# Reordering the beginning of a retention-plus-MLP kernel: table load, PSUM banks, early state terms, transfer order and half-width first columns

## The chip, the cores and the metric

One core of a Trainium2 chip runs the whole program. The metric is device microseconds for one execution. Engine names are those of the profile: PE (TensorE matmul), PEld (TensorE weight load), DVE (VectorE), ACT (ScalarE), POOL (GpSimd), SP (the engine that only issues transfers here).

## The reference

Inputs: q, k and v of 8 batches x 8 heads x 576 positions x 64, and two matrices, w_in (512 x 2048) and w_out (2048 x 512), all float32.

```python
scores = scale * np.matmul(q, k.transpose(0, 1, 3, 2))
gamma = 1.0 - 2.0 ** (-5.0 - np.arange(H))
Dmat = np.where(rel >= 0, gamma[:, None, None] ** rel[None, :, :], 0.0)   # rel = i - j
attn_out = np.matmul(scores * Dmat[None], v)                              # [8, 8, 576, 64]
x = attn_out.transpose(0, 2, 1, 3).reshape(B * S, H * D)                  # [4608, 512]
h = x @ w_in
out = (h * np.cos(h)) @ w_out                                             # [4608, 512]
```

The decay is a product of a factor of the query's position and one of the key's position, so the first part can be run as linear attention in chunks: within a chunk of 128 positions by masked scores, across chunks by a running 64 x 64 state for each head.

## The kernel before, in words

The program is written out by hand, instruction by instruction; there is no scheduler that moves anything. Each engine runs its own instructions in the order in which `emit` records them. The class `Sched` puts a wait in front of an instruction when a buffer (`Buf`) that it reads or writes was last touched by another engine. So the order of calls in `emit` is the order on every engine, and an instruction that waits holds up all that stands behind it on its engine.

**The long part.** The 4608 tokens are handled in 9 blocks of 512. For each block, `mlp1` makes 16 row tiles of h: four matmuls of 512 columns into one PSUM bank, then a cosine on ACT (a Sin with a bias of pi/2), then a product on DVE into `GT`. `mlp2` multiplies by w_out. The attention work of the next batches is put between these matmuls. There are eight PSUM banks: `mm0` to `mm3`, `sc0`, `sc1`, `po`, `st`.

**The beginning** is batch 0, and the change is only there (about 22 µs). It runs as follows.

- `load0` issues four pieces of k and four of q on SP (one for each pair of heads c), then `load` four chunks of v.
- `consts_a`, `consts_b`, `consts_n` make the masks and decay factors. `consts_b` runs four exponentials on ACT (the `up` factors, one for each c), and one buffer object, `bUP`, stands for all four. Behind them ACT loads a second function table for Sin (a one-element activation at line 694).
- `cast0` on POOL casts each piece to bf16 as it lands (k0, q0, k1, q1, ...). `vmul` on POOL multiplies each v chunk by its factors. Between these, `w_in_load` and `w_out_load` issue the matrices' transfers on POOL's queue, which also cast them to bf16. `WI` says how w_in's 16 column tiles are split over them: before, pieces of 2, 2, 4, 4 and 4 tiles.
- On PE, for each c: `turn0("k", c)` transposes k by 18 small matmuls, `back0(c - 1)` turns the result back into rows for the state, `turn0("q", c)` transposes q, `scores0(c - 1)` makes the masked scores of a pair of heads (eight matmuls, then two products on DVE at line 472). k's copies out of PSUM are on ACT (line 434, and 449 for `back0`), q's products with `up` on DVE (line 430). `spin(n, bank)` is n matmuls of the identity with itself, whose result nobody reads.
- `state(0, r)` adds chunk r to the running state in bank `st` and copies it out by two ACT instructions (line 585, buffer `SB[r]`). `sums(0, r)` makes chunk r's output: four matmuls of q with the state up to chunk r - 1, then eight of the masked scores with v; then one copy into `XT` (line 566), on ACT for even r and DVE for odd r.
- The fifth chunk of v and batch 1's k and v are loaded on SP behind the landing of w_in's last piece (`after=[w]`).
- Then come the 16 `mlp1` of block 0 and its `mlp2`.

Banks before: k's turns and `back0` go alternately to `mm0` and `mm1`, all q turns to `mm2`, the spins mostly to `st`.

Of the kernel before, what the change touches and what calls it, by code (L numbers as in the profile page):

```python
# [15 lines left out]
CH = 128  # L16
# [6 lines left out]
SP1 = 3 * 64 + CH  # L23
TQ = NP * S_
TP = 2 * TQ
WI = (0, 2, 4, 8, 12, 16)
NWO = 4


def ck_of(r):  # L30
    return min(CH, S_ - CH * r)
# [93 lines left out]
class _Kernel:  # L125
    def __init__(self, nc, es, q, k, v, w_in, w_out, out):
# [7 lines left out]
        def sb(name, shape, dt):  # L134
# [49 lines left out]
        self.MK = sb("mk", [128, CH], BF16)  # L184
        self.ID = sb("ident", [128, 128], BF16)
        self.LNG = sb("lng", [128, NP], F32)
        self.JUNK = sb("junk", [128, 1], F32)
        self.C_LN8 = sb("c_ln8", [128, 1], F32)
        self.C_PIH = sb("c_pih", [128, 1], F32)
        self.bIG, self.bIP, self.bUP, self.bWV, self.bMK, self.bC, self.bID, self.bUPN, self.bLW = (  # L190
            Buf() for _ in range(9))

        def ps(name):
            return nc.alloc_psum_tensor(name, [128, 512], F32)
# [31 lines left out]
    def consts_a(self):  # L226

        s = self.s
        s.op("pool", lambda e: e.iota(self.IP.ap(), [[CH, NCH]], base=0, channel_multiplier=1,
                                      allow_small_or_imprecise_dtypes=True), writes=[self.bIP])  # L230
        for t, b, fill, first, cmp in ((self.ID, self.bID, 1.0, 0.0, ALU.not_equal),
                                       (self.MK, self.bMK, 0.0, 1.0, ALU.is_ge)):
            s.op("dve", lambda e: e.memset(t.ap(), first), writes=[b])
            s.op("pool", lambda e: e.affine_select(t.ap(), t.ap(), pattern=[[1, CH]],
                                                   compare_op=cmp, fill=fill, base=0,
                                                   channel_multiplier=-1), reads=[b], writes=[b])
        for h in range(H_):
# [22 lines left out]
    def consts_b(self, c):  # L260

        s = self.s
        if c == 0:
            s.op("pool", lambda e: e.iota(self.IG.ap(), [[1, S_]], base=0, channel_multiplier=0,  # L264
                                          allow_small_or_imprecise_dtypes=True), writes=[self.bIG])
        s.op("act", lambda e: e.activation(  # L266
            bass.AP(self.UP, c * S_, [[NP * S_, 128], [1, S_]]), self.IG.ap(), AF.Exp,
            bias=self.C_LN8.ap(), scale=bass.AP(self.LNG, c, [[NP, 128], [1, 1]])),
            reads=[self.bIG, self.bC], writes=[Buf()])
        self.bUP.w = [Tok("act", "act", s.count["act"], {})]  # L270

# [138 lines left out]
    def turn_q(self, b, c, bank):  # L410
        s, i, n = self.s, b % 2, 9 * D_
        m, bm = bank
        f = self.turn9(m, lambda hp, t: bass.AP(
            self.QX[i], 64 * hp * NP * n + c * n + t * D_, [[NP * n, 64], [1, D_]]),
            [self.bQX[i]], bm)
        o = bass.AP(self.KQT[i], TQ + c * S_, [[TP, 128], [9, 64], [1, 9]])
        done = s.op("dve", lambda e: e.tensor_tensor(o, f, self.up9(c), ALU.mult),
                    reads=[bm, self.bUP], writes=[Buf()])
        for bq in self.bQT[i]:
            bq.w.append(done)  # L420

# [2 lines left out]
    def turn0(self, x, c, bank, eng):  # L424
        s, (m, bm) = self.s, bank
        f = self.turn9(m, lambda hp, t: self.rows0(x, c, 64, [t * D_, [1, D_]], hp),
                       [self.bX0[x][c]], bm)
        o = bass.AP(self.KQT[0], TQ * (x == "q") + c * S_, [[TP, 128], [9, 64], [1, 9]])
        if x == "q":
            fn = lambda e: e.tensor_tensor(o, f, self.up9(c), ALU.mult)  # L430
        elif eng == "dve":
            fn = lambda e: e.tensor_copy(o, f)
        else:
            fn = lambda e: e.activation(o, f, AF.Copy)  # L434
        done = s.op(eng, fn, reads=[bm] + [self.bUP] * (x == "q"), writes=[self.bT0[x][c]])
        for b in (self.bQT if x == "q" else self.bKT)[0]:
            b.w.append(done)

# [90 lines left out]
    def rest(self, b, r, po=None, eng="dve"):  # L529

        done = self.sums(b, r, po, eng)
        if r < NCH - 1:
            self.state(b, r)
        done()

    def sums(self, b, r, po=None, eng="dve"):

        s, ck, i, q0 = self.s, ck_of(r), b % 2, CH * r
        po, bpo = po or (self.PO, self.bPO)
        mms = []  # L540
        if r:
            sb = self.SB[(r - 1) % 3]
            mms += [(bass.AP(po, c * CH, [[512, 128], [1, ck]]),
                     bass.AP(sb, c * 128, [[512, 128], [1, 128]]),
                     bass.AP(self.KQT[i], TQ + c * S_ + q0, [[TP, 128], [1, ck]]),
                     dict(start=c == 0, stop=False, skip_group_check=True)) for c in range(NP)]
        for c in range(NP):
            for hp in range(2):
                h = 2 * c + hp
# [7 lines left out]
            reads += [x for bs in self.bR0 for x in bs]  # L557
        else:
            reads += self.bRT[self.rt[b, r]]
        if r:  # L560
            reads += [self.bSB[(r - 1) % 3], self.bQT[i][r]]
# [7 lines left out]
    def state(self, b, r):  # L569

        s, ck, i = self.s, ck_of(r), b % 2
        mms = []
        for c in range(NP):
            for hp in range(2):
                h = 2 * c + hp
                mms.append((
                    bass.AP(self.ST, 64 * hp * 512 + c * D_, [[512, 64], [1, D_]]),
                    bass.AP(self.KQB[i], 2 * DM * r + h * D_, [[NCH * 2 * DM, ck], [1, D_]]),
                    bass.AP(self.VB[i][r], h * D_, [[DM, ck], [1, D_]]),
                    dict(start=r == 0 and c == 0, stop=r == NCH - 2 and c == NP - 1,  # L580
                         skip_group_check=True)))
        self.group(mms, [self.bKB[i][r], self.bVB[i][r]], [self.bST])
        for hp in range(2):

            s.op("act", lambda e: e.activation(  # L585
                bass.AP(self.SB[r % 3], 64 * hp * 512 + 64 * hp, [[512, 64], [128, NP], [1, D_]]),
                bass.AP(self.ST, 64 * hp * 512, [[512, 64], [D_, NP], [1, D_]]), AF.Copy),
                reads=[self.bST], writes=[self.bSB[r % 3]] if hp else [Buf()])

    def stage(self, b, r):  # L590
        self.rest(b, r)
# [90 lines left out]
    def emit(self):  # L682
# [8 lines left out]
            self.consts_b(c)  # L691
        self.consts_n()

        s.op("act", lambda e: e.activation(self.JUNK.ap(), self.C_PIH.ap(), AF.Sin), reads=[self.bC])  # L694
        for c in range(NP):
            for x in "kq":
                self.cast0(x, c)
        self.vmul("pool", 0, 0)
        self.w_in_load(0)
        self.vmul("pool", 0, 1)  # L700
        self.vmul("pool", 0, 2)
        self.w_in_load(1)
        self.vmul("pool", 0, 3)
        for i in range(2, len(WI) - 1):
            w = self.w_in_load(i)
        for i in range(NWO):
            self.w_out_load(i)
            if i == 1:
# [2 lines left out]
        po, st = (self.PO, self.bPO), (self.ST, self.bST)  # L711
        mm, sc = list(zip(self.MM, self.bMM)), list(zip(self.SC, self.bSC))
        sc = [sc, [po, mm[3]]]
        self.spin(30, st)
        for c in range(NP):
            self.turn0("k", c, mm[c % 2], "act" if c else "dve")
            if c:
                self.back0(c - 1, mm[(c - 1) % 2])
            else:
                self.spin(4, st)  # L720
            self.turn0("q", c, mm[2], "dve")
            self.spin(4, st)
            if c:
                self.scores0(c - 1, sc[(c - 1) % 2])
        self.back0(3, mm[1])
        self.spin(8, mm[0])
        self.state(0, 0)
        self.scores0(3, sc[1])
        self.spin(4, mm[0])
        self.state(0, 1)  # L730
        self.spin(14, mm[2])
        self.state(0, 2)
        self.spin(14, mm[2])
        for r, bank in enumerate((mm[0], mm[1], mm[2], sc[0][0])):
            self.sums(0, r, bank, ("act", "dve")[r % 2])()
        self.state(0, 3)
        self.spin(6, po)
        self.n_mm = 3
        self.load("v", 0, NCH - 1, after=[w])
        self.vmul("pool", 0, NCH - 1)  # L740
# [3 lines left out]
        for r in range(NCH):  # L744
            self.casts(1, r)

        for dt in range(16):
            self.mlp1(0, dt)

        self.fetch(2)  # L750
# [96 lines left out]
```

## Time and profile before

| what | value |
|---|---|
| median of 3 runs (lowest to highest) | 314.74 µs (314.06 to 317.02) |
| the profiled execution's own time | 314.3 µs |
| its span, first to last instruction | 312.6 µs, so 1.7 µs lie around it |
| granted TensorE clock, mean | 1.00 |
| PE / PEld / DVE / ACT / POOL busy | 96% / 52% / 57% / 51% / 34% of the span |
| first `mlp1` weight load of block 0 | 22.09 µs from the span's start |
| PE busy before 22.09 µs | 17.58 of 22.09 µs |
| PE busy from 22.09 µs to the end | 283.92 of 290.51 µs |

Times inside the profile are microseconds from the span's start. A row of the timeline gives start, duration, engine, line, operation, output and inputs, and in brackets how long the engine was idle before and what released it. A row of the chain of waits gives start, duration and the work that the end of the program hung on at that moment; "issue" is time in which an engine waited for nothing that the profile shows. A row of a group gives the busy sum, the mean duration in ns, then the idle time before.

### The profile page before, as it was taken

Reading aid. Unit: us, or ns where it says so; the run is one execution under the profiler, and the core shown is the slowest. Engines: PE = TensorE matmul, PEld = TensorE weight load, DVE = VectorE, ACT = ScalarE, POOL = GpSimd, SP = SyncE. Lnnn points to the kernel's source line nnn. Section 1 sums busy time; section 2 is a strip of 40 time slices with the busy share of each in tenths; the row PEclk is TensorE's granted clock in tenths of the full one; section 3 lists DMA queues with packets and bytes.
Section 4 is the critical chain, followed back from the end, with each engine's and each line's share of the span. In section 5 each row is a group of like instructions: output and inputs, shape, how many; then the busy total and the mean of one; then the engine's idle time right before and its main releaser. Section 6 shows DMA issues by size and latency. Waiting matters only on the chain.

```text
span 312.6 us, 6548 instructions
## 1 busy us (share of the span) xinstructions
PE 301.5 (96%) x2578; PEld 162.2 (52%) x2614; DVE 176.8 (57%) x311; ACT 160.3 (51%) x283; POOL 107.8 (34%) x131
## 2 busy tenths in 40 slices
PE   7799999999999999999999999999999999999996
PEld 6564455666554555445544554455445554444444
DVE  4737644786547852685458554764487438405700
ACT  6657505775447533762367235723573247416711
POOL 5890017654657455645454654510000000000000
DMA  7999999999999999999999999940001100020012
GB/s 249 224 133 197 194 204 227 272 191 190 244 236 193 223 233 228 230 192 241 198 239 202 237 235 221 184 118 36 34 2 60 43 34 2 34 101 3 1 73 95
DMA packets 138846, 48.85 MB, mean 156 GB/s; under 512 B 127936, under 2 KB 133312, under 8 KB 138816
## 3 DMA queue, kind: packets, MB, share of 16 engines
q1 hardware_dynamic: 128352, 34.35, 58.3%
q0 software_dynamic: 5280, 4.78, 9.8%
q10 hardware_dynamic: 5184, 9.31, 8.2%
q8 instruction: 20, 0.33, 0.5%
q14 instruction: 10, 0.08, 0.1%
HBM read 36.70 MB, written 9.44 MB: 148 GB/s over the span
## 4 chain that ended last, share of the span: by engine, by line
PE 94%; ACT 3%; issue 2%; POOL 0%; DVE 0%; ACTq 0%
PE mm L491 63%; PE mm L493 21%; PE po L491 6%; PE sc L491 3%; PE st L491 2%; ACT up L266 1%; ACT L694 0%; ACT L266 0%; ACT kqb L449 0%; ACT sb L585 0%; DVE xt L566 0%; POOL ig L264 0%; ACT kqt L434 0%; PE st L493 0%; ACT osb L668 0%
## 5 line engine op out<-in xcount | busy, mean ns | idle before, releaser
L615 DVE TENSOR_TENSOR gt<-mm,cb 128x512 bf16<-128x512 f32 (+2 forms) x160 | 101.1, 637 | 62.4 <-ACT cb L612 61.1
L612 ACT ACTIVATE cb<-mm,c_pih 128x512 bf16<-128x512 f32 (+2 forms) x160 | 102.0, 644 | 30.3 <-PE mm L493 30.1
L491 PE MATMUL mm<-xt,win 128*128 128x512 bf16 (+2 forms) x470 | 116.6, 358 | 0.6 <-DVE xt L566 0.5
L491 PE MATMUL mm<-wout,gt 128*128 128x512 bf16 (+1 forms) x424 | 111.6, 372 | 3.0 <-issue 2.7
L491 PEld LDWEIGHTS mm<-xt,win 128*128 128x128 bf16 x480 | 45.5, 98 | 49.0 <-DVE gt L615 0.6
L491 PEld LDWEIGHTS mm<-wout,gt 128*128 128x128 bf16 x450 | 40.9, 98 | 42.0 <-DVE gt L615 0.2
L493 PE MATMUL mm<-xt,win 128*128 128x512 bf16 (+2 forms) x160 | 57.2, 358 | 0.4
L493 PE MATMUL mm<-wout,gt 128*128 128x512 bf16 (+1 forms) x142 | 53.6, 377 | 0.3
L649 ACT ACTIVATE osb<-mm 128x512 f32<-128x512 f32 x35 | 20.9, 597 | 62.8 <-PE mm L493 62.8
L339 POOL TENSOR_TENSOR vb<-vn,wv 128x512 bf16<-128x512 f32 (+1 forms) x40 | 41.6, 1041 | 30.0 <-DMA vn<-in_v_dram 28.2
L566 DVE CAST xt<-po 128x512 bf16<-128x512 f32 (+1 forms) x36 | 22.7, 630 | 41.8 <-PE po L493 41.8
L585 ACT ACTIVATE sb<-st 64x256 bf16<-64x256 f32 x64 | 24.1, 376 | 35.7 <-PE st L493 34.4
L339 POOL TENSOR_TENSOR kqb<-qn,upn 128x512 bf16<-128x512 f32 (+1 forms) x30 | 31.2, 1041 | 17.7 <-DMA qn<-in_q_dram 17.5
L350 POOL CAST kqb<-kn 128x512 bf16<-128x512 f32 (+1 forms) x35 | 21.3, 608 | 45.7 <-DMA kn<-in_k_dram 42.4
L518 DVE TENSOR_TENSOR rt<-sc,mk 128x512 bf16<-128x512 f32 (+1 forms) x52 | 29.2, 596 | 4.7 <-PE sc L493 4.7
L493 PEld LDWEIGHTS mm<-xt,win 128*128 128x128 bf16 x160 | 15.7, 98 | 15.7
L493 PEld LDWEIGHTS mm<-wout,gt 128*128 128x128 bf16 x142 | 13.9, 98 | 16.6
L491 PE MATMUL po<-rt,vb 128*64 128x128 bf16 (+1 forms) x252 | 14.0, 220 | 0.0
L518 DVE TENSOR_TENSOR rt<-mm,mk 128x512 bf16<-128x512 f32 x20 | 12.8, 678 | 0.0
L491 PEld LDWEIGHTS po<-kqt,sb 128*128 128x128 bf16 x116 | 8.3, 98 | 6.8 <-DVE rt L518 0.4
L491 PEld LDWEIGHTS po<-rt,vb 128*64 128x64 bf16 (+1 forms) x252 | 8.6, 108 | 5.6 <-DVE rt L518 2.1
L491 PE MATMUL po<-kqt,sb 128*128 128x128 bf16 (+1 forms) x116 | 10.4, 212 | 0.0
(115 smaller groups left out, 167.4 us busy)
## 6 DMA issues: line engine op xcount, KB each, us to landing
out_dram<-osb ACTq DMA_DIRECT2D x35, 256.0 KB, 3.4
vn<-in_v_dram SPq DMA_DIRECT2D x32, 256.0 KB, 5.4
kn<-in_k_dram SPq DMA_DIRECT2D x28, 256.0 KB, 4.5
qn<-in_q_dram SPq DMA_DIRECT2D x24, 256.0 KB, 4.8
wout<-in_moe_w_out_dram POOLq DMA_DIRECT2D x4, 512.0 KB, 18.4
win<-in_moe_w_in_dram POOLq DMA_DIRECT2D x3, 512.0 KB, 9.1
kn<-in_k_dram SPq DMA_DIRECT2D x4, 288.0 KB, 4.5
qn<-in_q_dram SPq DMA_DIRECT2D x4, 288.0 KB, 4.8
```

The costliest lines, as they stand in the source:

```text
L266: s.op("act", lambda e: e.activation(bass.AP(self.UP, c * S_, [[NP * S_, 128], [1, S_]]), self.IG.ap(), AF.Exp, bias=self.C_LN8.ap(), scal ...
L339: self.s.op(eng, lambda e: e.tensor_tensor(bass.AP(t, o, [[pitch, ck], [D_, H_], [1, D_]]), self.staged(x, r, [[D_, H_], [1, D_]]), bass.A ...
L350: fn = (lambda e: e.activation(o, f, AF.Copy)) if eng == "act" else (lambda e: e.tensor_copy(o, f))
L491: self.nc.tensor.matmul(o, a, b, **kw)
L493: return s.done("pe", self.nc.tensor.matmul(o, a, b, **kw), reads, writes)
L518: self.s.op("dve", lambda e: e.tensor_tensor(bass.AP(self.RT[k][hp], 0, p3), bass.AP(sc[0], 0, p3), bass.AP(self.MK, 0, [[CH, ck], [0, NP] ...
L566: fn = (lambda e: e.activation(o, f, AF.Copy)) if eng == "act" else (lambda e: e.tensor_copy(o, f))
L585: s.op("act", lambda e: e.activation(bass.AP(self.SB[r % 3], 64 * hp * 512 + 64 * hp, [[512, 64], [128, NP], [1, D_]]), bass.AP(self.ST, 6 ...
L612: s.op("act", lambda e: e.activation(co, mo, AF.Sin, bias=self.C_PIH.ap(), scale=1.0), reads=[bm, self.bC], writes=[bcb])
L615: s.op("dve", lambda e: e.tensor_tensor(bass.AP(g, dt * TB + o, [[16 * TB, 128], [1, n]]), mo, co, ALU.mult), reads=[bm, bcb], writes=bg[o ...
L649: s.op("act", lambda e: e.activation(o.ap(), m.ap(), AF.Copy), reads=[bm], writes=[bo])
```

## The change

Nothing is computed differently; eight edits move work in the beginning.

1. A one-element memset on DVE and a one-element Exp on ACT stand first in `consts_a`; the load of Exp's function table stands in front of this Exp and no longer behind the wait for the factors' inputs.
2. `bUP` becomes four buffers, one for each c.
3. Banks: k's turns all go to `mm0`, `back0` to `st`, q's turns alternate between `mm1` and `mm2`, the spins of this part go to `mm3`; there are fewer spins between the turns and others between the states.
4. `vmul` of chunk 2 of v goes from POOL to DVE, between the masked scores of c = 2 and of c = 3.
5. `WI` is 4, 4, 4, 4 tiles. On POOL's queue the order becomes: v0, w_in piece 0, v1, piece 1, v3, pieces 2 and 3, then w_out as before.
6. `sums` is split. `sums_q` (the four matmuls with the state) runs as soon as its state is copied out, in the gaps of the state chain; `sums_v` (the eight matmuls with v) runs after all states.
7. `state` gives back its copy-out as a function; that of chunk 3 is called after the first eight `mlp1`.
8. The first four row tiles of block 0 are made in two halves of 256 tokens: all four for the first half, then all four for the second, and the spin in front of them is gone.

```diff
-WI = (0, 2, 4, 8, 12, 16)
+WI = (0, 4, 8, 12, 16)
...
     def consts_a(self):
         s = self.s
+        bj = Buf()
+        s.op("dve", lambda e: e.memset(self.JUNK.ap(), 0.0), writes=[bj])
+        s.op("act", lambda e: e.activation(self.JUNK2.ap(), self.JUNK.ap(), AF.Exp), reads=[bj])
...
-            reads=[self.bIG, self.bC], writes=[Buf()])
-        self.bUP.w = [Tok("act", "act", s.count["act"], {})]
+            reads=[self.bIG, self.bC], writes=[self.bUP[c]])
...
     def sums(self, b, r, po=None, eng="dve"):
+        if r:
+            self.sums_q(b, r, po)
+        return self.sums_v(b, r, po, eng)
+
+    def sums_q(self, b, r, po=None):
+        ck, i, q0 = ck_of(r), b % 2, CH * r
+        po, bpo = po or (self.PO, self.bPO)
+        sb = self.SB[(r - 1) % 3]
+        self.group([(bass.AP(po, c * CH, [[512, 128], [1, ck]]),
+                     bass.AP(sb, c * 128, [[512, 128], [1, 128]]),
+                     bass.AP(self.KQT[i], TQ + c * S_ + q0, [[TP, 128], [1, ck]]),
+                     dict(start=c == 0, stop=False, skip_group_check=True)) for c in range(NP)],
+                   [self.bSB[(r - 1) % 3], self.bQT[i][r]], [bpo])
+
+    def sums_v(self, b, r, po=None, eng="dve"):
...
         self.group(mms, [self.bKB[i][r], self.bVB[i][r]], [self.bST])
-        for hp in range(2):
-            s.op("act", ...)
+        def evict():
+            for hp in range(2):
+                s.op("act", ...)
+        return evict
...
         self.vmul("pool", 0, 0)
         self.w_in_load(0)
         self.vmul("pool", 0, 1)
-        self.vmul("pool", 0, 2)
         self.w_in_load(1)
         self.vmul("pool", 0, 3)
-        for i in range(2, len(WI) - 1):
-            w = self.w_in_load(i)
+        self.w_in_load(2)
+        w = self.w_in_load(3)
...
-        self.spin(30, st)
+        self.spin(27, st)
         for c in range(NP):
-            self.turn0("k", c, mm[c % 2], "act" if c else "dve")
+            self.turn0("k", c, mm[0], "act" if c else "dve")
             if c:
-                self.back0(c - 1, mm[(c - 1) % 2])
+                self.back0(c - 1, st)
             else:
-                self.spin(4, st)
-            self.turn0("q", c, mm[2], "dve")
-            self.spin(4, st)
+                self.spin(4, mm[3])
+            self.turn0("q", c, mm[1 + c % 2], "dve")
+            if c < 2:
+                self.spin(4, mm[3])
             if c:
                 self.scores0(c - 1, sc[(c - 1) % 2])
-        self.back0(3, mm[1])
+        self.back0(3, st)
         self.spin(8, mm[0])
-        self.state(0, 0)
+        self.state(0, 0)()
+        self.vmul("dve", 0, 2)
         self.scores0(3, sc[1])
-        self.spin(4, mm[0])
-        self.state(0, 1)
-        self.spin(14, mm[2])
-        self.state(0, 2)
-        self.spin(14, mm[2])
-        for r, bank in enumerate((mm[0], mm[1], mm[2], sc[0][0])):
-            self.sums(0, r, bank, ("act", "dve")[r % 2])()
-        self.state(0, 3)
-        self.spin(6, po)
+        outs = [mm[0], mm[1], mm[2], sc[0][0]]
+        for r, n in ((1, 12), (2, 12), (3, 8)):
+            self.spin(n, mm[0])
+            if r < 3:
+                done = self.state(0, r)
+            self.sums_q(0, r, outs[r])
+            if r < 3:
+                done()
+        for r in range(NCH - 1):
+            self.sums_v(0, r, outs[r], ("act", "dve")[r % 2])()
+        done = self.state(0, 3)
...
-        for dt in range(16):
+        for o in (0, TB // 2):
+            for dt in range(4):
+                self.mlp1(0, dt, o, TB // 2)
+        done()
+        for dt in range(4, 16):
             self.mlp1(0, dt)
```

More of the change, by code (lines that the diff above doesn't have):

```diff
@@ L186, in __init__ @@
         self.LNG = sb("lng", [128, NP], F32)
-        self.JUNK = sb("junk", [128, 1], F32)
+        self.JUNK, self.JUNK2, self.JUNK3 = (sb(f"junk{i}", [128, 1], F32) for i in range(3))
         self.C_LN8 = sb("c_ln8", [128, 1], F32)
         self.C_PIH = sb("c_pih", [128, 1], F32)
-        self.bIG, self.bIP, self.bUP, self.bWV, self.bMK, self.bC, self.bID, self.bUPN, self.bLW = (
-            Buf() for _ in range(9))
+        self.bIG, self.bIP, self.bWV, self.bMK, self.bC, self.bID, self.bUPN, self.bLW = (
+            Buf() for _ in range(8))
+        self.bUP = [Buf() for _ in range(NP)]
         def ps(name):
@@ L417, in turn_q @@
         done = s.op("dve", lambda e: e.tensor_tensor(o, f, self.up9(c), ALU.mult),
-                    reads=[bm, self.bUP], writes=[Buf()])
+                    reads=[bm, self.bUP[c]], writes=[Buf()])
         for bq in self.bQT[i]:
@@ L434, in turn0 @@
             fn = lambda e: e.activation(o, f, AF.Copy)
-        done = s.op(eng, fn, reads=[bm] + [self.bUP] * (x == "q"), writes=[self.bT0[x][c]])
+        done = s.op(eng, fn, reads=[bm] + [self.bUP[c]] * (x == "q"), writes=[self.bT0[x][c]])
         for b in (self.bQT if x == "q" else self.bKT)[0]:
@@ L532, in rest @@
         if r < NCH - 1:
-            self.state(b, r)
+            self.state(b, r)()
         done()
     def sums(self, b, r, po=None, eng="dve"):
+        if r:
[11 more added lines that the diff above has]
+    def sums_v(self, b, r, po=None, eng="dve"):
         s, ck, i, q0 = self.s, ck_of(r), b % 2, CH * r
@@ L540, in sums @@
         mms = []
[L541 to L546, printed above, removed]
         for c in range(NP):
@@ L559, in sums @@
             reads += self.bRT[self.rt[b, r]]
-        if r:
-            reads += [self.bSB[(r - 1) % 3], self.bQT[i][r]]
         self.group(mms, reads, [bpo])
@@ L582, in state @@
         self.group(mms, [self.bKB[i][r], self.bVB[i][r]], [self.bST])
-        for hp in range(2):
[L585 to L588, printed above, removed]
+        def evict():
+            for hp in range(2):
+                s.op("act", lambda e: e.activation(
+                    bass.AP(self.SB[r % 3], 64 * hp * 512 + 64 * hp, [[512, 64], [128, NP], [1, D_]]),
+                    bass.AP(self.ST, 64 * hp * 512, [[512, 64], [D_, NP], [1, D_]]), AF.Copy),
+                    reads=[self.bST], writes=[self.bSB[r % 3]] if hp else [Buf()])
+        return evict
     def stage(self, b, r):
@@ L692, in emit @@
         self.consts_n()
-        s.op("act", lambda e: e.activation(self.JUNK.ap(), self.C_PIH.ap(), AF.Sin), reads=[self.bC])
+        s.op("act", lambda e: e.activation(self.JUNK3.ap(), self.C_PIH.ap(), AF.Sin), reads=[self.bC])
         for c in range(NP):
```

## The prediction

> **What bounds the kernel now.** The page first: the span and the chain.
>
> ```profile
> span 312.6 us, 6548 instructions
> ...
> q8 instruction: 20, 0.33, 0.5%
> ...
> PE 94%; ACT 3%; issue 2%; POOL 0%; DVE 0%; ACTq 0%
> ```
>
> The end hangs on PE. The stages split it at the first `mlp1`: before 22.09 us PE is busy 17.58 us (much of it spins), behind it 283.92 of 290.51. PE's waits behind it are 2.7 us of "issue" in 17 small pieces, 0.5 and 0.2 us for DVE; none is for a transfer. So the change can move only the 22.09 us, and what it saves there shifts all the rest, as long as weights keep ahead. Next the chain of waits inside the beginning:
>
> ```profile
> 2.33 1.28 ACT L266
> 3.62 0.01 issue
> 3.63 3.15 ACT up L266 x4
> ...
> 7.14 1.28 ACT L694
> ...
> 8.63 0.54 ACT kqt L434
> 9.17 0.50 ACT kqb L449
> ...
> 13.07 0.71 issue
> ...
> 14.70 0.61 ACT kqb L449
> ...
> 21.34 0.70 DVE xt L566
> ```
>
> ACT's two table loads and four exponentials hold the chain until 8.63; k1's copy (L434) is late by that, then PE until 14.70, then the states. Last the timeline:
>
> ```profile
> 13.77 0.10 PEld L493 LDWEIGHTS st<-ident 128*128 128x128 bf16 x1 [0.88 <-issue]
> 14.26 1.04 POOL L339 TENSOR_TENSOR vb<-vn,wv 128x512 bf16<-128x512 f32 x1 [0.27 <-DMA vn<-in_v_dram]
> 22.09 0.33 PEld L491 LDWEIGHTS mm<-xt,win 128*128 128x128 bf16 x3 [0.40 <-DVE xt L566]
> ```
>
> The first row is a stall amid four spins without any wait. The third: the first `mlp1` waits for the last XT copy.
>
> **The change, part by part.**
>
> *Tables.* The first load starts when ACT is released, near 0.95 (DVE's first row is at 0.89), and not at 2.33 behind the iota. With a small Exp (0.20, as L694's) the factors start at 2.45 instead of 3.63. ACT keeps 3.15 + 0.22 + 0.22 for them and 1.28 + 0.20 for Sin: free at 7.5, not 8.63 (-1.15). The added memset (0.06, as L241's) delays the identity by as much; the first transposes wait for POOL's cast of k0 (4.43), so it costs nothing.
>
> *Factors apart.* q0's product waited 0.9 us for all four factors (6.88); now it starts at 5.8. That frees DVE, not the chain.
>
> *Banks.* k2's turn waited 1.0 us for `kqb` of c = 0 in `mm0`; now only for k1's copy. ACT does a copy (0.64) and a `kqb` (0.59) per c, back to back from 7.5. POOL's casts end at 8.19 (k2), 9.66 (k3), 10.45 (q3); a turn takes 0.5. Followed step by step: k1's copy 7.5 to 8.15, `kqb0` to 8.75, k2's turn 8.6, its copy to 9.75, `kqb1` to 10.35, k3's turn 10.15, its copy to 11.35, `kqb2` to 11.95, `back0(3)` to 12.4, `kqb3` to 13.1. Before, it ended at 15.30. That would be -2.2.
>
> *The stall.* 20 packets in 0.33 MB are 16 KB each, on a queue of kind "instruction". 2614 weight loads and as many matmuls make 5228 instructions, about 260 for a packet, or 130 matmuls. The first packet starts in the window 11.0 to 11.5; the stall ends at 13.77. In the program's order it stands before matmul 222, the next boundary is then about matmul 350, and a packet is asked for a block ahead: matmul 222 - 128 = 94 is q1's turn, at 7.69 before and about 7.5 after. I read this as code that arrives late. After, matmul 222 is at the end of `back0(3)`: 27+18+4+18+4 spins and turns for c = 0, then 52, 48, 48, then `back0`. PE gets there at 12.4 and, if the packet comes as it did, waits until about 13.6 (from 13.4, as it is asked for 0.2 to 0.3 earlier, to 13.77). `kqb3` then runs 13.8 to 14.4, and state 0 starts at 14.45 instead of 15.35: -0.9. That is my value; with no stall it is -2.2.
>
> The Trainium skill says against it (Runtime: NRT & Kernel Launch, Instruction fetch mechanics) that code comes in blocks of 256 instructions and that crossing one is mostly hidden. The row of 0.71 says not here; by the page the sum below would be 1.3 us better.
>
> *States.* A round of state, copy-out and semaphores took 1.19 (16.54 to 17.73). From 14.45: states at 14.45, 15.7 (twelve spins end there), 16.9, last copy-out to 18.05. q's matmuls take 0.33 for a chunk (19.21 to 19.54), v's 0.34. Those of q now lie in the gaps, but for the last: 18.1 to 18.4. Four times 0.34 ends at 19.8, state 3 takes 0.27, and no XT copy of chunk 3 stands before the first half: XT of chunk 1 is done at 19.8 (0.69 on DVE). First `mlp1` at 20.1. So 15.35 to 22.09 (6.74) becomes 5.6: -1.1.
>
> *v2 on DVE.* The nearest rows are DVE's product from PSUM (0.69) and POOL's own (1.04); I take 0.7. DVE ends the masks of c = 2 at 14.15 and v2 lands at 14.26, so it runs to 14.95. Behind it stand the two masks of c = 3 (1.3), whose scores come at 15.05: done 16.4, needed 18.4. Hidden by 2 us; even 1.04 costs nothing. POOL is rid of 1.04; v3's product moves from 16.06 to between 15.0 and 15.7.
>
> *w_in.* The pieces land (issue plus landing): 256 KB at 11.99 + 4.3 = 16.3; 512 KB at 17.05 + 6.3 = 23.4, the last at about 29.4 (it released SP). Now 512 KB go out at 11.99, 14.0, about 16.6 and 17.4. Piece 0 costs 4.3 to 6.3: 16.3 to 18.3, needed at 20.1. Later pieces are issued up to 3 us sooner than the same tiles before and land near 20, 22.5 and 25, needed at 23.6, 27.0, 30.5. w_out, issued behind, moves up too. SP's v4 and batch 1 hang on the last piece and follow it from 25. Nothing added; cover about 2 us.
>
> *Halves.* Eight half tiles cost PE the same 3.46. ACT's cosine of 256 columns lies between 0.419 (192) and 0.526 (320): 0.47; DVE's product between 0.352 and 0.486: 0.42. ACT with its gap needs 0.49 a half against PE's 0.43, and the copy-out of state 3 (0.78) stands behind. PE runs four banks ahead, so PE loses 0.1 to 0.2 (0.5 with 0.526); in full tiles ACT (0.69 of 0.86) catches up. +0.15.
>
> Sum: -0.9 - 1.1 + 0.15 = -1.85. The profiled run took 314.3 (span 312.6 + 1.7): 312.45, told as 312.4. It lies 0.4 below the median of 314.74, inside the runs shown; the sum is made from it. One per cent of the median, 3.1 us, is about what a measurement of this kernel can tell from no change.
>
> One more rule speaks against fewer spins: the Trainium skill (TensorE: Matmul & The Clock Gate, Part 1) halves PE's clock after an idle window of some 3.4 us. Here 12 early spins take 1.46 us and 13 later ones 0.73, so a slow phase exists, but the longest gap I expect is 1.2 us, as the 1.2 before 9.77 which slowed nothing.
>
> **The rivals.**
>
> *The code is there in time* (22%). The stall is not fetch-bound or the packet comes sooner. Then state 0 starts at 13.15, v1 is ready at 13.99, and the chain ends 1.3 us earlier: 311.1. For: PE asks earlier and the packet lies on a loaded DMA only by chance. Against: k, q and v load the DMA just as before 11 us.
>
> *The gain is eaten in part* (21%). ACT's halves at 0.526, or v2 and v3 late behind a piece 0 of twice the size (v2 beyond 15.6 counts), or a stall to 14.2. Each costs 0.4 to 1.2: 312.9 to 314.0, say 313.6. For: transfers filled 0.97 of the DMA from 10 to 20 us. Against: the covers above.
>
> *The next block of code is late* (6%), the other side. It is asked for when the stall ends, 13.6, and matmul 350 is the first `mlp1`, at 20.1. Before, the wait from boundary to packet was 3.4 us (7.69 to 11.06), then 1.3 (13.77 to the packet after 15.0), then 3.1 (20.97 to one after 23.8); the packet takes about 1.3 and PE resumes 1.4 behind it. With 3.4 it arrives at 19.7, in time. Beyond 3.8 PE stands still at the first `mlp1`, beyond 5.7 the kernel is slower than before; with 7 it is 315.6. For: two pieces of 512 KB now fill the DMA in that window. Against: no row reaches 3.8.
>
> **How the numbers follow.** The forecast has 51%, its own range 311.6 to 313.2 (stall end 13.4 to 14.0, halves 0 to 0.5, v2 on DVE). The range reaches to the first two rivals: 310.9 to 314.2. Faster by over 1% (below 311.6) holds most of the first rival and the forecast's edge: 0.25. Slower by over 1% needs a block more than 8.8 us late: 0.03. The rest, 0.72.
>
> **What would show it.** Right: ACT's first table load near 0.95 and the factors near 2.45; k2's turn near 8.6; a stall "issue" of about 1.2 us inside `back0(3)`, ending near 13.6; state 0 near 14.45; first `mlp1` near 20.1 with no wait for XT or w_in; cosines of 256 columns near 0.47. Wrong: no stall there (then 311.1), a wait of the first `mlp1` for a transfer or for code, or new PE waits behind it for w_in or w_out.

## The result, and the profile after

| kernel | median of its runs (lowest to highest) | ratio of the times, 95% interval |
|---|---|---|
| before | 314.54 µs (313.76 to 318.5) | 1 |
| changed | 312.94 µs (311.15 to 314.91) | 0.9942 (0.9921 to 0.9964) |

The changed kernel is 0.6% faster, which is inside the 1% that was called no change. The profiled execution took 313.94 µs (span 312.2), so it is 1.0 slower than the median; its profile shows why. Line numbers have moved: the spins and turns are now at L494 and L496 (before L491, L493), `kqt` and `kqb` on ACT at L437 and L452, v's product at L342, the XT copy at L578, the copy-out of the state at L599.

The page of the changed kernel, its span and the chain that ended last:

```profile
span 312.2 us, 6598 instructions
...
PE 93%; DMA 3%; SPq 1%; POOL 1%; issue 1%; ACT 0%; DVE 0%
```

ACT had 3% of the chain before and has 0% now; DMA has 3% in its place. The chain of waits in the beginning, same execution, says which transfer:

```profile
4.71 8.30 DMA vn<-in_v_dram
...
13.09 1.04 POOL vb L342
14.13 0.86 POOL win L321
...
15.01 1.07 POOL vb L342
...
19.69 0.70 DVE xt L578
...
20.43 0.28 PE mm L494
20.72 1.13 issue
```

The tables, copies and turns that stood here until 14.70 are off the chain. State 0 now hangs on the landing of v's first chunk (13.01) and its product, and behind the first matmul of the long part there are 1.13 µs in which PE waits for nothing that the profile shows. The timeline has the rows that answer to the forecast's steps (ACT, POOL, DVE and PE in turn):

```profile
0.81 1.28 ACT L232 ACT_TABLE_LOAD   x1 [0.81 <-PEq L854]
2.39 3.15 ACT L270 ACTIVATE up<-ig,c_ln,lng 128x576 f32<-128x576 f32 x4
7.30 0.63 ACT L437 ACTIVATE kqt<-mm 128x576 bf16<-128x576 bf16 x1
7.86 0.67 POOL L305 CAST qx<-qn 128x576 bf16<-128x576 f32 x1 [1.55 <-DMA qn<-in_q_dram]
13.09 1.04 POOL L342 TENSOR_TENSOR vb<-vn,wv 128x512 bf16<-128x512 f32 x1 [1.52 <-DMA vn<-in_v_dram]
14.72 2.46 DVE L342 TENSOR_TENSOR vb<-vn,wv 128x512 bf16<-128x512 f32 x1
14.27 0.29 PE L494 MATMUL st<-vb,kqb 128*64 128x64 bf16 x7 [0.56 <-POOL vb L342]
20.43 0.28 PE L494 MATMUL mm<-xt,win 128*128 128x256 bf16 x1 [0.22 <-DVE xt L578]
21.85 0.39 PE L494 MATMUL mm<-xt,win 128*128 128x256 bf16 x2 [1.13 <-issue]
22.39 3.61 ACT L627 ACTIVATE cb<-mm,c_pih 128x256 bf16<-128x256 f32 x8 [1.84 <-PE mm L496]
```

In the profile of before, state 0 and the first `mlp1` (rows of PE) read:

```profile
15.35 0.31 PE L491 MATMUL st<-vb,kqb 128*64 128x64 bf16 x7 [0.24 <-ACT kqb L449]
...
22.32 0.59 PE L491 MATMUL mm<-xt,win 128*128 128x512 bf16 x2 [0.45 <-DVE xt L566]
```

Of the changed kernel's rows, the first three are the table edit: ACT is free for k1's copy at 7.30 instead of 8.54. The next two show transfers that came later than in the profile of before (q1's cast at 7.86, there 6.76; v0's product at 13.09, there 11.00). The state starts at 14.27 and not at 15.35, the first `mlp1` at 20.43 and not at 22.32 (its matmul). Of these 1.9 µs the stall at 21.85 takes 1.13. By the order of the program that stall stands before PE's 349th matmul, where the forecast had put a block's boundary ("about matmul 350").

### The profile page after: what moved, and what is told of

The parts are those of the page before. It is cut to its first block, busy times and chain, and to the rows that moved or that the text cites. A ratio compares the mean times of both kernels' runs of the same rounds, so it can differ in the third digit from the quotient of the medians.

```text
span 312.2 us, 6598 instructions
## 1 busy us (share of the span) xinstructions
PE 304.3 (97%) x2613; PEld 163.0 (52%) x2613; DVE 179.6 (58%) x317; ACT 161.2 (52%) x288; POOL 106.2 (34%) x129
## 4 chain that ended last, share of the span: by engine, by line
PE 93%; DMA 3%; SPq 1%; POOL 1%; issue 1%; ACT 0%; DVE 0%
PE mm L494 63%; PE mm L496 20%; PE po L494 5%; PE sc L494 3%; DMA vn<-in_v_dram 3%; PE st L494 1%; SPq L293 1%; POOL vb L342 1%; PE po L496 1%; POOL win L321 0%; ACT sb L599 0%; DVE xt L578 0%; ACT osb L683 0%; PE st L496 0%; PE sc L496 0%
## 5 line engine op out<-in xcount | busy, mean ns | idle before, releaser
L630 DVE TENSOR_TENSOR gt<-mm,cb 128x512 bf16<-128x512 f32 (+3 forms) x164 | 101.7, 626 | 62.5 <-ACT cb L627 59.5
L494 PE MATMUL mm<-xt,win 128*128 128x512 bf16 (+3 forms) x492 | 119.2, 353 | 1.4 <-issue 1.1
L627 ACT ACTIVATE cb<-mm,c_pih 128x512 bf16<-128x512 f32 (+3 forms) x164 | 102.8, 636 | 30.3 <-PE mm L496 29.8
L494 PE MATMUL mm<-wout,gt 128*128 128x512 bf16 (+1 forms) x450 | 117.4, 373 | 0.0
L494 PEld LDWEIGHTS mm<-xt,win 128*128 128x128 bf16 x492 | 46.4, 98 | 49.5 <-issue 1.3
L494 PEld LDWEIGHTS mm<-wout,gt 128*128 128x128 bf16 x450 | 40.9, 98 | 42.1 <-DVE gt L630 0.2
L496 PE MATMUL mm<-xt,win 128*128 128x512 bf16 (+3 forms) x164 | 57.9, 353 | 0.0
L496 PE MATMUL mm<-wout,gt 128*128 128x512 bf16 (+1 forms) x142 | 53.6, 378 | 0.0
L342 POOL TENSOR_TENSOR vb<-vn,wv 128x512 bf16<-128x512 f32 (+1 forms) x39 | 40.9, 1048 | 28.9 <-DMA vn<-in_v_dram 28.3
L578 DVE CAST xt<-po 128x512 bf16<-128x512 f32 (+1 forms) x36 | 22.7, 630 | 41.7 <-PE po L496 41.7
L599 ACT ACTIVATE sb<-st 64x256 bf16<-64x256 f32 x64 | 24.1, 377 | 36.5 <-PE st L496 35.2
L342 POOL TENSOR_TENSOR kqb<-qn,upn 128x512 bf16<-128x512 f32 (+1 forms) x30 | 31.3, 1042 | 18.0 <-DMA qn<-in_q_dram 16.6
L496 PEld LDWEIGHTS mm<-xt,win 128*128 128x128 bf16 x164 | 16.0, 98 | 15.3
L496 PEld LDWEIGHTS mm<-wout,gt 128*128 128x128 bf16 x142 | 13.9, 98 | 16.5
L494 PE MATMUL po<-rt,vb 128*64 128x128 bf16 (+1 forms) x252 | 14.0, 220 | 0.0
L494 PEld LDWEIGHTS po<-rt,vb 128*64 128x64 bf16 (+1 forms) x252 | 8.6, 108 | 5.6 <-DVE rt L521 2.1
L494 PEld LDWEIGHTS po<-kqt,sb 128*128 128x128 bf16 x87 | 7.1, 98 | 6.5 <-issue 0.2
L494 PE MATMUL sc<-kqt 64*128 64x128 bf16 (+1 forms) x196 | 10.3, 213 | 0.0
```

What stands on the lines that cost most here:

```text
L342: self.s.op(eng, lambda e: e.tensor_tensor(bass.AP(t, o, [[pitch, ck], [D_, H_], [1, D_]]), self.staged(x, r, [[D_, H_], [1, D_]]), bass.A ...
L494: self.nc.tensor.matmul(o, a, b, **kw)
L496: return s.done("pe", self.nc.tensor.matmul(o, a, b, **kw), reads, writes)
L578: fn = (lambda e: e.activation(o, f, AF.Copy)) if eng == "act" else (lambda e: e.tensor_copy(o, f))
L599: s.op("act", lambda e: e.activation(bass.AP(self.SB[r % 3], 64 * hp * 512 + 64 * hp, [[512, 64], [128, NP], [1, D_]]), bass.AP(self.ST, 6 ...
L627: s.op("act", lambda e: e.activation(co, mo, AF.Sin, bias=self.C_PIH.ap(), scale=1.0), reads=[bm, self.bC], writes=[bcb])
```

## The experiments

All comparisons are with runs of the kernel before taken alongside on the same chip (three series, medians 314.49, 314.57 and 314.48). Beside the times, one reading is used throughout: the weight loads of two traces are paired, counted from the end of the program, and the difference of their start times is the shift at that place. Against the profiled execution of before, in µs:

| kernel | first `mlp1` matmul at | shift at 33 µs | at 53 µs | at the end |
|---|---|---|---|---|
| before | 22.32 | 0 | 0 | 0 |
| before, again | 21.70 | -0.38 | +0.18 | +0.19 |
| changed | 20.43 | -0.29 | -0.29 | -0.38 |
| changed, again | 19.67 | -2.36 | -2.36 | -2.46 |
| changed, w_in's old pieces | 20.36 | -1.67 | -1.51 | -1.61 |
| changed, v2 on POOL | 20.49 | -1.54 | -1.54 | -1.64 |
| changed, wide spins | 19.38 | -2.65 | -2.65 | -2.75 |
| wide, banks undone | 19.11 | -2.79 | -2.79 | -2.89 |
| wide, tables undone | 19.13 | -2.90 | -2.40 | -2.50 |
| wide, halves undone | 19.36 | -2.73 | -2.72 | -2.67 |
| wide, q by state undone | 19.16 | -2.70 | -2.70 | -2.80 |
| wide, three edits undone | 21.49 | -0.82 | -0.82 | -0.93 |
| before, wide spins | 21.54 | -0.50 | -0.19 | +0.09 |
| before, banks alone | 21.23 | -1.09 | -0.08 | -0.08 |

Each line is one execution. That with three edits undone took 313.37 µs (its kernel's median is 312.39), that of before with wide spins 314.37 (median 313.53).

**The changed kernel once more.** 

> The changed kernel itself, once more. Theory A (the beginning now hangs on landings): the landing of v0 (13.04 in the first profile, 10.96 before) and of q1 (7.84, before 6.74) differ from run to run, and the first mlp1 moves with them, 19 to 20.5; times spread over 311 to 314.5. Theory B (fixed costs of the change: v2's product at 2.46 us on DVE, halves): landings do not matter, first mlp1 again at 20.4 and the span again near 312.

Measured 312.39 µs, ratio 0.9932 (0.9914 to 0.995). v's first chunk landed at 11.74 (13.01 in the first profile), v2's product on DVE took 0.93 instead of 2.46, and the first `mlp1` came at 19.67, inside the 19 to 20.5 of the first theory. The timeline, PE's rows that waited:

```profile
13.18 0.23 PE L496 MATMUL st<-ident,kqt 128*128 128x128 bf16 x1 [0.28 <-issue]
14.10 0.31 PE L494 MATMUL st<-vb,kqb 128*64 128x64 bf16 x7 [0.24 <-ACT kqb L452]
19.67 0.50 PE L494 MATMUL mm<-xt,win 128*128 128x256 bf16 x3 [0.22 <-DVE xt L578]
```

The stall is inside `back0(3)`, 0.28 where the forecast had about 1.2; state 0 waits for `kqb`, and nothing stops the first `mlp1`. Of the first profile's two waits (v's landing, and code at the first `mlp1`) neither is there: they differ from execution to execution.

**Spins as 512-column matmuls.** Each four spins of the beginning become one matmul of 512 columns, so PE gets fewer instructions for the same time.

```diff
-        self.spin(27, st)
+        self.spinw(7, st)
...
-        self.spin(8, mm[0])
+        self.spinw(2, mm[0])
-        for r, n in ((1, 12), (2, 12), (3, 8)):
-            self.spin(n, mm[0])
+        for r, n in ((1, 3), (2, 3), (3, 2)):
+            self.spinw(n, mm[0])
```

> The spins of the beginning as a quarter as many matmuls of 512 columns (same PE time, about 60 matmuls and 60 weight loads fewer). Theory A with late code: matmul 350 now stands about 62 matmuls into the mlp1 part, reached 8 to 10 us later than the first mlp1, so the stall of 1.13 us at the second matmul of the first mlp1 is gone: about 1.1 us less, near 311.8. Rival: the stall belongs to the place (w_in's landing, a bank) and stays at the first mlp1; no change, 312.9.

Measured 311.47 µs, ratio 0.9902 (0.9885 to 0.9918): below both kernels. PE's waits before 24 µs (engine, line, what it waited for, us in total, times, longest):

```profile
PE st L500 <- POOL ident L238: 1.5, 1, 1.5
PE mm L500 <- POOL gt L305: 0.9, 1, 0.9
PE st L500 <- ACT kqb L452: 0.4, 2, 0.3
PE mm L500 <- DVE xt L584: 0.2, 1, 0.2
```

No wait for code is left. A packet still came 5.5 µs behind its boundary (15.25 to 20.71), but with fewer instructions the next boundary was reached only at 28.5. That is one part of the answer; another is in the clock, below.

**w_in's old pieces.** `WI` is 2, 2, 4, 4, 4 again, the rest as changed.

> w_in in pieces of 2, 2, 4, 4, 4 tiles again, the rest of the change kept. Theory A: with 256 KB pieces the second block of code comes 1 to 3 us after matmul 222 as before (1.3) and not 6.5, no stall at the first mlp1; but tiles 2 and 3 of the first halves hang on piece 1 (issue near 16, landing near 19.5, needed at about 21.3). Time 0.5 to 1.1 less, near 312.2. Rival: the packet is late whatever the pieces; stall of about 1 stays, 312.9 or, with a wait for piece 1, up to 313.5.

Measured 312.94 µs, ratio 0.9956 (0.994 to 0.9972). PE's rows inside `back0(3)` and after:

```profile
13.86 0.23 PE L496 MATMUL st<-ident,kqt 128*128 128x128 bf16 x1 [0.92 <-issue]
...
14.78 0.31 PE L494 MATMUL st<-vb,kqb 128*64 128x64 bf16 x7 [0.24 <-ACT kqb L452]
```

This is the stall that the forecast had drawn, at the place it named and 0.3 late. The larger first piece does not cause it: the packet that PE waits for there came at 10.93 to 12.21, and w_in's first piece was issued at 12.84. The packet behind it is another matter. It came 2.4 µs behind its boundary here, and nothing stopped the first `mlp1`. Over all profiles this second lag is 0.3 to 2.6 µs in the five with the old pieces, and 0.5 to 6.5 in the nine with the larger ones, above 5 in five of them. So the larger pieces may delay it; one profile for each kernel does not show it.

**v2's product back on POOL.**

> v2's product back on POOL behind v1's, the rest of the change kept. Theory A: DVE's 2.46 us were hidden (the masks of c = 3 ended 0.6 us ahead of v's matmuls), while POOL now issues pieces 1 to 3 some 1.04 later and state 2 waits for POOL: same to 0.7 slower, 312.9 to 313.6. Theory B: the 2.46 us were the loss: masks of c = 3 end about 1.5 us earlier and the kernel is 0.5 to 1 us faster, near 312.2.

Measured 312.6 µs, ratio 0.9937 (0.9913 to 0.9961): no difference from the changed kernel that these intervals could show. What this run taught is elsewhere. Its profiled execution has a mean granted clock of 0.995; the windows 5.5 to 8.9, 8.9 to 12.3 and 12.3 to 15.7 show where (the column behind POOL's busy time is the granted clock):

```profile
5.50:8.90 3.40, 2.20 (x66) 1.74 (x65) 1.27 (x3) 3.00 (x7) 1.76 (x3) 0.94 1.03 379
8.90:12.30 3.40, 3.40 (x74) 2.58 (x75) 2.59 (x4) 1.14 (x2) 2.81 (x5) 0.56 1.09 231
12.30:15.70 3.40, 2.98 (x79) 2.31 (x74) 3.40 (x7) 2.18 (x5) 3.38 (x5) 1.00 0.76 131
```

For 3.4 µs PE ran at half clock, in the middle of k's and q's turns: the window 8.51 to 11.92 alone has a granted clock of 0.50. Half of 3.4 µs is 0.55% of the span, so a mean clock of 0.995 marks one such spell. Read by this mark, the timed runs of all kernels divide as follows.

| kernels | runs with a clock of 0.995 or less | median of these | median of the others |
|---|---|---|---|
| before (three series) | 10 of 51 | 316.0 | 314.4 |
| changed, and changed again | 10 of 28 | 313.8 | 312.1 |
| all with wide spins (seven kernels) | 1 of 48 | 312.5 | 312.1 |

A spell costs about 1.6 µs (1.6 before, 1.7 after). The change made spells no rarer (10 of 28 against 10 of 51; 12 of 30 in the three other kernels that have its smaller number of narrow spins), if anything more frequent, and the wide spins all but removed them. The mark misses one thing: every profiled execution starts slowly (before: the first 29 spins take 3.0 µs, 13 later ones 0.73), and how long that lasts is not in the mean (see three edits undone, below). Without a spell, the changed kernel is 2.3 faster than before (312.1 against 314.4).

**The kernel before, once more.** 

> The kernel before, one more profile. Theory A (landings scatter from run to run by chance): q1 lands anywhere in 6.7 to 7.8 and v0 in 11 to 13, as with the changed kernels (7.5 to 7.8 and 11.7 to 13.0), and its first mlp1 stays within 0.3 of 22.09, since its chain hangs on ACT until 9.7. Rival: the change itself slows k's and q's transfers, q1 lands at 6.7 and v0 at 11.0 again.

Measured 314.49 µs. q1 landed at 7.38 and v's first chunk at 11.56 (6.71 and 10.93 in the first profile), so landings scatter without the change too. It reached the first `mlp1` 0.6 earlier than in the first profile and was no faster for it. Its waits between 24 and 60 µs:

```profile
PE po L491 <- POOL kqb L350: 0.4, 1, 0.4
```

Batch 1's first k was cast too late, and the 0.4 gained in the beginning were lost again at 46.9 µs (shift -0.38, then +0.18).

**One edit undone at a time, with wide spins.** Tables and factors (edits 1 and 2) as before; halves (edits 7 and 8) as before; q by state (edit 6) late, together with v's matmuls.

> The kernel with wide spins (311.47), with edits 1 and 2 undone: no early Exp, one buffer for the four factors; so the table load waits for the iota again and ACT is free at 8.6. Theory A (the chain hangs on the landings of k and q): k1's copy moves from 8.15 to 8.65, but k2's and k3's casts end at 8.9 and 10.4 as before and the last kqb moves by 0.2 or less: 311.5 to 311.8. Rival (the first step of my forecast, ACT's 1.15 us are on the path): +0.9 to 1.1, near 312.5.

> The kernel with wide spins (311.47), with the halves undone (edits 7 and 8): state 3 copied out at once, one wide spin, 16 full mlp1. The first mlp1 waits for chunk 3's copy again: it ends 0.6 to 0.7 after that of chunk 1, and the forecast's 0.15 for ACT comes back: +0.4 to 0.6, near 312.0. Rival: ACT's halves cost as much as they save, 311.5.

> The kernel with wide spins (311.47), with edit 6 undone: q's matmuls stand with v's again, behind all states. Three times 0.33 come behind the last copy-out, of which 0.33 had to be there anyway and the rest lay in gaps: +0.6 to 0.7, near 312.1. Rival: the last copy-out and the masks set the start of v's matmuls so late that the gaps take it all, 311.5.

Measured 312.12 (ratio 0.9907, 0.988 to 0.9934), 311.97 (0.9904, 0.988 to 0.9929) and 311.59 (0.9896, 0.9869 to 0.9923), against 0.9902 with all edits in. None of them alone is worth as much as an interval (0.65, 0.5 and 0.1 µs by the medians). With the tables undone 0.5 of the gain went between 33 and 53 µs, where PE waited 0.24 for batch 1's k: this wait can come back when the gain is large enough. The table edit does not even show in the beginning: ACT's first copy is at 8.55 and yet the first `mlp1` is at 19.13, since PE's own order and POOL's casts set the pace of k2's and k3's turns.

**Three edits undone together, wide spins.** The same three, at once; banks, POOL's order and v2 on DVE stay.

> Wide spins, with tables, separate factors, halves and early q by state all undone together; banks, order on POOL's queue and v2 on DVE stay. One by one these three cost 0.6, 0.5 and 0.1 us or nothing. If they cover for one another (each gain hidden as long as the others are there), together they cost more than the sum of 1.2: 313 or above, first mlp1 beyond 20.5. If they are small for good reason, 311.6 to 312.7, first mlp1 near 19.7.

Measured 312.39 µs, ratio 0.9937 (0.9913 to 0.9961). Together they are worth 0.9 µs by the medians. That is less than the three single losses added up (1.3): in the times they do not cover for one another, and of the two expectations the second (311.6 to 312.7) has the time right. In the profiles the loss is 1.8 at the end (-0.93 against -2.75), but that execution took 313.37, one of two slower ones among six, and its rows say why. q1's turn in it, and below in the changed kernel with wide spins:

```profile
8.32 0.69 PE L499 MATMUL mm<-ident,qx 64*64 64x64 bf16 x17
```

```profile
8.37 0.47 PE L500 MATMUL mm<-ident,qx 64*64 64x64 bf16 x17
```

A turn takes 0.68 to 0.69 inside the spell of half clock above, and 0.47 at full clock. In this execution turns take 0.66 to 0.69 up to the one at 10.02 and 0.47 from 11.08 on, while in the other thirteen profiles the slow stretch ends, at the latest, during a turn that starts at 6.95. So PE was at half clock until about 10.9, and the mean granted clock of 0.999 does not tell it. The first `mlp1` at 21.49 instead of 19.38, and state 0 at 14.60 instead of 13.68, therefore cannot be put down to the edits. What lies behind state 0, at full clock, can: to the first `mlp1` it is 6.89 instead of 5.70.

**Banks undone, wide spins.**

```diff
-            self.turn0("k", c, mm[0], "act" if c else "dve")
+            self.turn0("k", c, mm[c % 2], "act" if c else "dve")
             if c:
-                self.back0(c - 1, st)
+                self.back0(c - 1, mm[(c - 1) % 2])
...
-            self.turn0("q", c, mm[1 + c % 2], "dve")
+            self.turn0("q", c, mm[2], "dve")
```

> The changed kernel with wide spins and with edit 3 undone: k's turns and back0 alternate between mm0 and mm1 again, every q turn is in mm2, the spins between turns in st. If the banks carry the gain (k2's turn then waits for kqb of c = 0 again, about 1.0 us, and every later turn with it), the first mlp1 comes at 20.4 instead of 19.4 and the time is about 312.6. If it is the code (fewer instructions, so no block boundary is met while its packet is missing), the banks are worth nothing while ACT and the casts set the pace: about 311.6, first mlp1 near 19.4.

Measured 311.25 µs, ratio 0.989 (0.9864 to 0.9916), the lowest of all, though not to be told from the 0.9902 with the banks parted. With everything else in place, the banks are worth nothing: k3's copy starts at 11.37 without them and at 11.40 with them.

**The kernel before with wide spins alone.** 

> The kernel before with wide spins alone, none of the eight edits. If the stall on code and the small spins were the main loss, it comes near the changed kernel: about 312.3 to 312.8, first mlp1 near 20. If the edits carry the gain, only the stall of 0.3 to 0.7 us goes: about 314.0, first mlp1 near 21.3.

Measured 313.53 µs, ratio 0.9966 (0.9945 to 0.9986), and a clock of 1.0 in all 12 runs. It is neither of the two numbers expected, but between them. No spell and no wait for code remained, and still 2 µs are missing to the changed kernel with wide spins. The kernel with three edits undone divides them: 1.1 from here to it (banks, v2 on DVE, w_in's pieces and order), 0.9 from it to all edits. The 1.1 do not seem to be won in the beginning: the two profiles, 0.8 and 1.0 above the medians of their kernels, reach the first `mlp1` at 21.54 and 21.49.

**The kernel before with the banks alone.** Edit 3 and nothing else.

> The kernel before with edit 3 alone (banks and fewer spins between turns). If the banks carry the gain: k2's turn no longer waits for kqb, first mlp1 1.0 to 1.5 earlier, about 313.2. If the banks only move the wait to the code's block or to the factors, about 314.4, first mlp1 near 21.7 to 22.

Measured 314.15 µs, ratio 0.9988 (0.9972 to 1.0004): no difference that the interval shows. Five of its 12 runs have a spell; the median of the others is 313.87 against 314.4 before, so up to half a microsecond may arrive. The profile shows where the rest goes. Its timeline, PE's rows that matter:

```profile
13.34 0.23 PE L493 MATMUL st<-ident,kqt 128*128 128x128 bf16 x1 [0.51 <-issue]
...
14.26 0.31 PE L491 MATMUL st<-vb,kqb 128*64 128x64 bf16 x7 [0.24 <-ACT kqb L449]
...
40.51 0.28 PE L491 MATMUL po<-kqt,sb 128*128 128x64 bf16 x4 [0.85 <-POOL vb L339]
```

State 0 starts at 14.26 instead of 15.35: 1.09 in the beginning, as forecast (0.70 against the 14.96 of the kernel before again). At 40.51 PE waits 0.85 for v's fifth chunk, and the shift falls from -1.09 to -0.08. POOL's timeline of this kernel, and below it of the one with three edits undone, which keeps edits 4 and 5 (v2 on DVE; w_in's four pieces and their order):

```profile
39.33 1.03 POOL L339 TENSOR_TENSOR vb<-vn,wv 64x512 bf16<-64x512 f32 x1 [16.19 <-DMA vn<-in_v_dram]
45.85 0.61 POOL L350 CAST kqb<-kn 128x512 bf16<-128x512 f32 x1 [5.49 <-DMA kn<-in_k_dram]
```

```profile
35.66 1.03 POOL L341 TENSOR_TENSOR vb<-vn,wv 64x512 bf16<-64x512 f32 x1 [14.24 <-DMA vn<-in_v_dram]
42.85 0.61 POOL L352 CAST kqb<-kn 128x512 bf16<-128x512 f32 x1 [6.16 <-DMA kn<-in_k_dram]
```

Without edits 4 and 5 (before twice, and the two kernels built on it) v's fifth chunk is multiplied at 38.4 to 39.3 and batch 1's k cast at 45.0 to 46.2. In the ten profiles with one or both of them it is 35.7 to 37.9 and 42.2 to 44.5. These transfers wait on SP for w_in's last piece, which lands at 29.0 to 30.0 without the two edits and at 26.6 to 29.0 with them. In the profile of before PE took up the fifth chunk 1.2 after POOL's product ended (38.36 + 1.03):

```profile
40.58 0.28 PE L491 MATMUL po<-kqt,sb 128*128 128x64 bf16 x4
```

A gain of more than 1.2 in the beginning had to run into it. So edits 4 and 5, which shorten nothing in the beginning, are what lets the gain reach the end. Their shares were not parted: v2 back on POOL, with POOL's order as before but four pieces, has 35.7 and 42.2; the old five pieces, with v2 on DVE, have 36.7 and 44.5.

## Why the prediction came out as it did

The time was right (312.4 told, 312.94 measured, a median that mixes 312.1 without and 313.8 with a spell of half clock). There was some luck in it: without spells the gain was 2.3 and not 1.85, and the spells, which the forecast had dismissed, hid the difference. Its reasons were right in part:

- *Tables*: right in the row (free at 7.30, told 7.5), but of little worth alone (0.25 by the profiles and 0.65 by the medians in the run with the edit undone, less than its interval).
- *Banks and the stall*: told -0.9, with `back0(3)` stalled until about 13.6 and state 0 at 14.45. k2's turn came at 9.65 in the first profile (told 8.6), since q1 and k2 landed later. State 0 came at 14.27, 14.10 and 14.78 in the three profiles with narrow spins and v2 on DVE. The stall was there in the second and third (0.28 and 0.92), and in the kernel with the banks alone (0.51). In the first profile v0's late landing (13.01, 10.93 before) took its place. The forecast took landings from one execution as fixed; that of v's first chunk scatters by 2 µs over the profiles.
- *States*: told -1.1. From state 0 to the first `mlp1` matmul it was 6.97 before and 5.57 in the second profile: -1.4. By the weight load, which the forecast used, it is 6.74 and 5.57: -1.2. The undone edits agree (6.89 without q early and halves).
- *Halves*: told +0.15. A cosine took 0.45 (3.61 for 8), told 0.47. From the first `mlp1` matmul to 33 µs the second profile lost 0.29 (-2.65 to -2.36), but the kernel with the halves undone lost 0.23 on the same way (-2.96 to -2.73). So the halves themselves cost about 0.06.
- *v2 on DVE*: told 0.7, and "even 1.04 costs nothing". It took 2.46 in the first profile, with POOL's product of v1 (15.01) and an issue of w_in (15.99) beside it, 0.93 in the second and 0.69 with wide spins. The masks ended at 18.38, told need 18.4: the cover of 2 µs was used to the end, and held.
- *w_in*: "Nothing added" missed a term. The forecast asked whether the later transfers would still come in time, and not what the old ones would take from a gain: waits of 0.85 at 40.5 in the kernel with the banks alone and of 0.41 at 46.9 in the kernel before. Edits 4 and 5 were worth more than "nothing", as the 1.1 above shows (with the banks, which are worth nothing where they were undone alone).
- *The next block of code late* (6%): "no row reaches 3.8" was a bound from three waits. In the first profile after, the packet came 6.5 µs after its boundary (13.03 to 19.54) and PE stood still for 1.13 at the first `mlp1`, as that rival had it. That execution was still no slower than the profiled one of before (313.94 against 314.3). In the changed kernel again and in the one with w_in's old pieces the lag was 1.4 and 2.4 at this place. The Trainium skill's "mostly hidden" (Runtime: NRT & Kernel Launch, Instruction fetch mechanics) does not hold for PE here while the inputs load: stalls of 0.28, 0.51, 0.92 and 1.13, and 0.71 before.
- *Fewer spins*: the forecast weighed the rule against it and dismissed it, since "the longest gap I expect is 1.2 us, as the 1.2 before 9.77 which slowed nothing". This step failed. In the run of v2 on POOL the spell came without any idle time above 0.69 from 4.5 to 8.5; PE was busy for 2.21 of the 3.41 µs ahead of it (5.10 to 8.51). The same stretch of the changed kernel again has 2.37 and no spell. The Trainium skill (TensorE: Matmul & The Clock Gate, Part 1) has the window's length right (3.4 µs here too), but its table of states speaks of an idle window, and this one was two thirds full. Its Part 4 adds that transposes do not count as busy in the same way. k's and q's turns are transposes, so that would fit, but no run here changed them.

Summed for an execution without spell or long stall: state 0 -1.25 (15.35 to 14.10), states -1.4, +0.3 from the first `mlp1` to 33 µs, and -0.1 after 53 µs, which is -2.46 in the second profile after. Told: -1.85. The difference to the median of 312.94 is in part the share of runs with a spell; three of the changed kernel's 22 runs with a full mean clock are above 313.9 too, the profiled one with its late landing and stall among them.

Three things stay open. Three runs of the kernel before with wide spins (above 314.1 against 313.5) have a full mean clock, and one of them is the profiled one; their cause was not found. Which part of edits 4 and 5 brings the transfers forward was not parted. And the wide spins change both the number of PE's instructions and the rows that PE is fed, so how much of their 0.9 µs (312.39 to 311.47) is code and how much clock was not parted.

## What to carry to other kernels

A gain at the start is worth only what the next transfer with a fixed landing leaves of it: look, before counting it, how long every later input has been ready when it is first used, and move its issue up by as much. Edits of a few tenths each show nothing one by one; undo them together before calling them useless, and add up the single losses before saying that they cover for one another. Before reading a profile against another, compare the time that the same matmuls take in both: a mean clock of 0.999 did not tell that one had started at half clock for longer. Few and wide warm-up matmuls are worth trying: here they covered the same time with a quarter of the instructions, ended the waits for code in the profiles, and left 1 of 48 runs with a spell.

## What the hardware did that was not expected

- The code packet for PE's next block came 0.3 to 6.5 µs after the boundary that asks for it (the second of each profile). PE went on 1.35 after the late packet's end (20.50 to 21.85).
- One half-clock spell of 3.4 µs came in 10 of 51 runs before, 10 of 28 after and 1 of 48 with wide spins, and cost about 1.6 µs.
- The half clock at the start lasted until about 10.9 µs in one execution, although PE was busy for 3.26 of the 3.42 µs from 4.08 to 7.50; in the other thirteen profiles it ended, at the latest, during a turn that starts at 6.95.
- The same DVE product of 128x512 took 0.69, 0.93 and 2.46 µs in three executions. The long one ran beside POOL's product and an issue of POOL's queue; no run separated the two.
- The landing of v's first chunk lay between 10.93 and 13.01 µs in fourteen profiles, all but one below 11.8, with the same issues ahead of it.
